# Linear attention and an MLP-mixer block in one program: batch 0's token order, fp32 key transposes, batch 1's numerators, and a new order table

## The chip, the core and the metric

The kernel runs on one core of a Trainium2 chip. A core has five engines that run side by side, each with its own instruction queue: TensorE (PE: matmuls from SBUF into PSUM, with weight loads, PEld, beside them), VectorE (DVE), ScalarE (ACT), GpSimd (POOL) and SyncE (SP), which here only issues transfers. POOL and ACT issue transfers too. The metric is the time of one execution on the device in microseconds (us); lower is better.

## The reference

Eight batches, eight heads, 576 tokens, head size 64, 128 random features. The attention is linear: queries and keys become positive features, and the sum over tokens is taken once for each head. Its result, with the heads side by side (512 channels), goes through a mixer block: an MLP over the tokens (576 to 256 to 576) with a residual, then one over the channels (512 to 1536 to 512) with a residual.

```python
def phi(x):
    proj = np.einsum('bhsd,md->bhsm', x, omega)
    sq = np.sum(x * x, axis=-1, keepdims=True) / 2.0
    h = proj - sq
    h = h - np.max(h, axis=-1, keepdims=True)
    return np.exp(h) / np.sqrt(m)
q_p, k_p = (phi(q_s), phi(k_s))
kv = np.einsum('bhsm,bhsd->bhmd', k_p, v)
z = np.sum(k_p, axis=2)
num = np.einsum('bhsm,bhmd->bhsd', q_p, kv)
den = np.einsum('bhsm,bhm->bhs', q_p, z)[..., None] + 1e-06
# attention out: num / den; then, x being (batch, tokens, channels):
h = np.maximum(xt @ w_tok1, 0.0) @ w_tok2      # xt: x with tokens last
u = x + h.transpose(0, 2, 1)
h2 = np.maximum(u @ w_ch1, 0.0) @ w_ch2
return (u + h2).astype(np.float32)
```

Inputs and output are fp32 in the chip's main memory.

## The kernel before

**Tiling.** Matmul operands are fp16, sums are fp32 in PSUM. The tokens of a batch are cut into 512 main tokens and 64 tail tokens. A main token stands at partition p and place j with token = 4p + j, so one transfer brings four neighbouring tokens to a partition. The tails of two batches share a partition range, and all eight tails go through the channel MLP as a ninth piece at the end (`channel_mix(B, ...)`).

**Stages of a batch.** First q and k are brought with the head size on the partitions. For batches 0 and 1 TensorE does it: `transposes` and `tail_transposes` (L465, L485) write a PSUM bank, ScalarE or VectorE copies it to `kT` or `qT` (L470, L472, L489). For batches 2 to 7 POOL issues a transfer that casts to fp16 in main memory (L354), and SP two transposing ones (L362). Then `attention`, by pairs of heads:

- kp: key features on TensorE (L611), exp on ScalarE (L494); qp: the same for queries (L625).
- km: VectorE takes the maximum over the features (L637) and its reciprocal; vs: POOL scales v with it (L644).
- kv: TensorE sums over tokens (L657, L664), a copy to `kvsb` (L672).
- num: numerators and denominators on TensorE (L691, L693), then reciprocal and product on VectorE into `x` (L700, L701). Batch 0 does one head at a time in one of six PSUM banks; all others do two heads at once in the only two-bank buffer, `pair`.

The tails have their own smaller steps (kt, L526 and L538 or L494; qt, L586; vbd on POOL, L545 or L571). Then comes `token_mix` (L728 to L748, then a transposing transfer from `u` to `uT`, L753) or, for batch 0, `token_mix_first`: it computes u already transposed, in four blocks of 128 channels (L771, L772: w_tok1; L787: x through an identity matmul; L789: w_tok2; L793: the copy to `uT`). At last `channel_mix`: twelve blocks against w_ch1 (L822; for the first two blocks of batch 0 three quarters ahead, L828, and the last quarter later, L830), relu on ScalarE (L839), then four output pieces against w_ch2 (L855), the residual (L864; batch 0 adds it by an identity matmul, L853, and copies at L861), and the store from SP (L869; L872 for the ninth piece).

In `token_mix_first` the 512 columns of the moving operand w_tok2 are read in the order of (j, p), which is a step of four elements in memory:

```python
def w2_of(tb, j=None):
    rows = w2[:, tb, 0:SM].rearrange("p (c j) -> p j c", j=NJ)
    return rows if j is None else rows[:, j, :]
```

**Start of batch 0.** Keys come as fp32 in four pieces of two heads over the queues of ACT and SP (`load_first`, L377) into space that later holds w_ch2. ScalarE casts each to fp16 (L381), and then they are transposed. Everything else comes over POOL's queue. POOL's transfers are chained in the order in which the code names them (`job.after`): the tails and q and v of batch 0, w_tok1, w_tok2, half of w_ch1, batch 1's k, the other half of w_ch1, batch 1's q and v, the two halves of w_ch2 (L442), and then batch 2.

**The order.** Every step is a job with an engine, an estimated cost, the jobs that it needs, the buffers that it takes and gives, and a key. A planner written in the kernel (`Planner.run`) walks through time with those estimates: on each engine, of the jobs that could begin first, the one with the lowest key comes next. Each engine then runs its jobs in that order. Keys come from tables: `HEAD` for batch 0, one entry for each head or block; `NEAR` for batches 1 and 2; `KEYS` for the rest. `BY` says for some copies of batch 0 whether ScalarE (A) or VectorE (D) does them. Where the planner sees TensorE idle before the first channel mix, it puts in matmuls of zeros (`warm`, L908); they compute nothing that is used.

Of the kernel before, what the change touches and what calls it, by code (L numbers as in the profile page):

```python
# [16 lines left out]
KEYS = {"a": -1.383, "as": 0.1, "t": -0.936, "ts": 0.381, "gv": 2.163, "lt": -2.027, "lv": -2.126, "to": -1.882, "tt": 0.315, "ks": 0.333, "km": 0.498, "vs": -0.625, "l1": -2.543, "kt": -0.025}  # L17
NEAR = {"1": {"a": -1.493, "as": 0.086, "t": -1.525, "ts": 0.0, "gv": -0.107, "km": -1.714, "vs": -0.23, "kt": -0.097}, "2": {"a": -1.272, "as": 0.154, "t": -0.7, "ts": 0.142, "gv": 1.686, "km": 3.516, "vs": 1.881, "lv": -1.598, "lt": -2.533, "kt": 0.06}}
HEAD = {"kp": [-3.838, -3.822, -3.798, -3.404], "ke": [-2.728, -2.927, -2.827, -2.727], "km": [-4.011, -3.564, -4.193, -4.006], "vs": [-3.332, -3.487, -3.03, -3.14], "qp": [-3.503, -3.403, -3.303, -3.203], "qe": [-3.328, -3.374, -3.028, -3.128], "kv": [-3.45, -3.145, -2.92, -3.05], "ko": [-3.015, -2.969, -3.397, -2.755], "n": [-3.199, -3.199, -3.182, -3.099, -2.999, -2.999, -2.899, -2.899], "no": [-3.34, -3.34, -3.24, -3.058, -3.14, -4.038, -3.04, -2.3], "ktm": -3.64, "kt": -5.015, "kte": -3.991, "qt": -3.751, "qte": -4.062, "kx": [-6.595, -5.9, -5.8, -5.7], "kxo": [-6.013, -7.195, -5.8, -5.71], "ktx": -6.15, "ktxo": -5.5, "qx": [-5.449, -2.792], "qxo": [-4.557, -3.081], "qtx": -5.58, "qtxo": -3.371, "t1": [-0.475, -0.755, -0.539, -0.445], "re": [-0.554, -0.394, -0.244, -0.084], "ut": [-0.17, -0.48, -0.32, -0.64], "uo": [-0.453, -0.293, -0.302, 0.017], "vbd": -8.94, "w1": -9.59, "w1t": -9.68, "w2t": -8.94, "wa": -8.32, "wb": -8.79, "w2": -8.13}
BY = {"kx": "DDDD", "ktx": "A", "qx": "AD", "qtx": "D", "ko": "ADDA", "re": "AADA", "uo": "DAAA", "no": "DDDDDDDD"}  # L20
# [157 lines left out]
def kernel(  # L178
# [37 lines left out]
    def sb(shape, dt, name):  # L216
        return pool.tile(shape, dt, name=name)
# [13 lines left out]
    omT = sb([P, M], FP16, "omT")  # L231
    ident16 = sb([P, P], FP16, "ident16")
# [142 lines left out]
    def load_first(h0, h1, eng, key, to):  # L375
        def go():
            (nc.sync if eng == "SP" else nc.scalar).dma_start(  # L377
                out=first_k[:, h0:h1, :], in_=k[0, h0:h1, 0:SM, :].rearrange("h (p j) d -> p h (j d)", j=NJ))
        got = dma(eng, key, 0.37 * (h1 - h0), go, cost=0.47)
        def cast():  # L380
            (nc.vector.tensor_copy if to == "DVE" else nc.scalar.copy)(out=nat["k", 0][:, h0:h1, :], in_=first_k[:, h0:h1, :])  # L381
        job = add(to, 0.6 if to == "DVE" else 0.5, key + 0.1, cast, deps=[got])
        for h in range(h0, h1):
            ld["k", 0, h] = job

    def identities():
        make_identity(nc, ident16)
    j_ident = add("POOL", 0.45, -9.9, identities)
    j_om = [dma("SP", -9.95, 0.1, lambda: nc.sync.dma_start(out=omega_nat, in_=omega))]
    load_first(0, 2, "ACT", -9.9, "ACT")  # L390
    load_first(2, 4, "SP", -9.9, "ACT")
    load_first(4, 6, "ACT", -9.7, "ACT")
    load_first(6, 8, "SP", -9.7, "ACT")
# [27 lines left out]
    def w2_of(tb, j=None):  # L421
        rows = w2[:, tb, 0:SM].rearrange("p (c j) -> p j c", j=NJ)
        return rows if j is None else rows[:, j, :]
# [35 lines left out]
    def transposes(b, w, h0, h1, key, on_act=False, key_out=None):  # L459
        name = ("t", w, b, h0)  # L460
        def go():
            ps, ident = bank16(name), ident16
            for i in range(2 * (h1 - h0)):
                h, pr = h0 + i // 2, i % 2
                nc.tensor.transpose(ps[:, i * P : (i + 1) * P], nat[w, b][:, h, pr * P : (pr + 1) * P], ident)  # L465
        def out_():
            n = h1 - h0
            ps = bank16(name)[:, 0 : n * R].rearrange("p (h r) -> p h r", h=n)
            if on_act:
                nc.scalar.copy(out=rows_of(b, w)[:, h0:h1, 0:R], in_=ps)  # L470
            else:
                nc.vector.tensor_copy(out=rows_of(b, w)[:, h0:h1, 0:R], in_=ps)  # L472
        take = [("bank", name)]
        take.append((w + "T", b))
        t = add("PE", mm(2 * (h1 - h0), P) * 1, key, go, deps=[ld[w, b, h0], j_ident], take=take)
        e = add("ACT" if on_act else "DVE", 0.1 + 0.21 * (h1 - h0) if on_act else 0.16 + 0.13 * (h1 - h0), key if key_out is None else key_out, out_, deps=[t], give=[("bank", name)])
        for h in range(h0, h1):
            tr[w, b, h] = e
# [19 lines left out]
    def attention(b, key, step):  # L498
# [95 lines left out]
        for hp in range(NU):  # L594
# [75 lines left out]
            kv_act = b > 0 or BY["ko"][hp] == "A"  # L670
# [8 lines left out]
            for hs in ((0,), (1,)) if b == 0 else ((0, 1),):  # L679
                n_h = (n_n, hs)  # L680
                at = ("bank" if b == 0 else "pair", n_h)
                def where(n_h=n_h, hs=hs):
                    return bank(n_h).unsqueeze(1) if b == 0 else pair(n_h)
# [35 lines left out]
        return last_x, j_start  # L719

    def token_mix(b, key, step, jx):
# [35 lines left out]
        uT.append(dma("SP", key + step * 0.95, 2.6, ut_dma, deps=ju, take=[("uT", b)], cost=3.5))  # L757
        return jr, uT

    def token_mix_first(b, key, step, jx):  # L760

        jrs, uT = [], []
        for db in range(ND):
# [20 lines left out]
            def ut_(n2=n2, cols=cols):  # L784
                ps, x, r1 = bank(n2), t_x[place("x", b)], t_r1[place("r1", b)]
                for j in range(NJ):
                    nc.tensor.matmul(ps[:, j * P : (j + 1) * P], x[:, j, cols], ident16, start=(j == 0), stop=False, skip_group_check=True)  # L787
                for tb in range(NT):
                    nc.tensor.matmul(ps, r1[:, tb, cols], w2_of(tb), start=False, stop=(tb == NT - 1), skip_group_check=True)  # L789
# [23 lines left out]
    def channel_mix(c, key, jt):  # L813
# [3 lines left out]
        for cb in range(NCB):  # L817
# [20 lines left out]
            def relu(cb=cb, n=n):  # L838
                nc.scalar.activation(out=t_r3[place("r3", c)][:, cb, :], in_=bank(n), func=AF.Relu)  # L839
            jr.append(add("ACT", 0.5, key + 0.5 * cb / NCB, relu, deps=[j1], take=[("r3", c)], give=[("bank", n)]))  # L840
        for j in range(NJ):
            last = c == B and j == NJ - 1
            for hf in range(2 if last else 1):
                n = ("h4", c, j, hf)
                cols = slice(hf * (DM // 2), (hf + 1) * (DM // 2)) if last else slice(0, DM)
                prev = None
                for part in range(3):
# [8 lines left out]
                    prev = add("PE", mm(4, 256 if last else 512) + (mm(4, P) if c == 0 and part == 2 else 0.0), key + 0.5 + 0.5 * (3 * j + part) / 12 + 0.2 * hf, c2,  # L856
# [8 lines left out]
                jo = add("DVE", 0.4 if last else 0.69, k2, oadd, deps=[prev], take=[("o", (c, j))], give=[("bank", n)] + ([("u", c)] if 0 < c < B else []))  # L865
                def store(j=j, cols=cols, last=last):
                    o = t_o[place("o", (c, j))]
                    if c < B:
                        nc.sync.dma_start(out=out[c, 0:SM, :].rearrange("(p j) d -> p j d", j=NJ)[:, j, :], in_=o)  # L869
# [22 lines left out]
    for b in range(B):  # L892
        if b >= NPE:
            load_transposed(b, b + key_of("lt", b), [touched.get(b - 2)])
            load_v_tail(b, b + key_of("lt", b) + 0.02)
            load_v(b, b + key_of("lv", b), [ld["ktt", b]])
# [44 lines left out]
```

The softmax here doesn't subtract the row's maximum and nothing guards it: scores larger than these inputs give would overflow.

## Time and profile before

| What | Value |
|---|---|
| Median of 3 runs | 292.88 us |
| Lowest and highest | 292.81 and 293.12 us |
| The profiled execution: its time | 292.57 us |
| its span, first to last instruction | 290.8 us |
| TensorE busy | 283.9 us, 98% of the span |
| ScalarE, VectorE, POOL busy | 155.9, 145.3 and 90.6 us |
| Mean granted TensorE clock | 0.997 |
| Bytes moved by transfers | 39.57 MB |

The profile is of one execution. Times count from its first instruction. The rows name the engine, the line of the code, the operation, and what it writes and reads; a group's row gives its busy time and the mean duration of one in nanoseconds. The duration of a single matmul includes the time that it takes to run through the array, so it overlaps with the next one; the spacing of matmuls is read from the chain of work that ended last, which gives the start, the length and the count of each piece. Counted as busy are also the matmuls of zeros.

### The profile page before, as it was taken

How to read it: one execution, taken by the hardware profiler on the slowest of the kernel's cores; microseconds unless marked ns; L12 is line 12 of the kernel's file. 1: busy time of each engine (PE TensorE's matmuls, PEld its weight loads, DVE VectorE, ACT ScalarE, POOL GpSimd, SP SyncE). 2: the span in 40 equal slices, each digit the busy share in tenths (PEclk: the TensorE clock that was granted, in tenths of full speed). 3: DMA queues.
4: the chain of work that ended last, by engine and by line, in shares of the span. 5: the costliest groups of instructions: out<-in, count | busy, mean ns of one | idle time of the engine just before them, and what ended most of it. 6: DMA issues, size and time to landing. Idle time of an engine off the chain costs nothing.

```text
span 290.8 us, 5502 instructions
## 1 busy us (share of the span) xinstructions
PE 283.9 (98%) x2210; PEld 141.7 (49%) x2210; DVE 145.3 (50%) x269; ACT 155.9 (54%) x305; POOL 90.6 (31%) x115
## 2 busy tenths in 40 slices
PE   7899999999999999999999999999999999999994
PEld 3465454445544544465445544554455444444443
DVE  4885843558449533756567446646465242111011
ACT  5963992098457553865466636753765501621700
POOL 8995740128006501550165014601421000000000
PEclk9999999999999999999999999999999999999998
DMA  8999999699964996999769976897711033003004
GB/s 192 193 197 195 202 228 172 98 246 175 177 108 108 186 152 125 180 171 202 113 129 182 197 114 113 159 221 115 152 72 39 0 72 147 0 18 144 2 20 124
DMA packets 75737, 39.57 MB, mean 136 GB/s; under 512 B 54976, under 2 KB 70720, under 8 KB 75328
## 3 DMA queue, kind: packets, MB, share of 16 engines
q0 software_dynamic: 24304, 17.43, 41.2%
q1 hardware_dynamic: 50624, 21.01, 32.3%
q10 hardware_dynamic: 784, 0.79, 0.9%
q8 instruction: 17, 0.28, 0.4%
q14 instruction: 8, 0.07, 0.1%
HBM read 35.88 MB, written 16.52 MB: 180 GB/s over the span
## 4 chain that ended last, share of the span: by engine, by line
PE 95%; ACT 3%; DVE 0%; issue 0%; DVEq 0%; ACTq 0%
PE bank L855 33%; PE bank L822 32%; PE bank L745 4%; PE bank L728 4%; PE bank L611 3%; PE bank L657 3%; PE bank L625 2%; PE pair L691 2%; PE bank L908 2%; ACT kp L494 1%; PE bank L789 1%; PE bank L803 1%; PE bank L664 1%; PE bank L465 1%; PE bank L729 1%; ACT qp L494 1%
## 5 line engine op out<-in xcount | busy, mean ns | idle before, releaser
L839 ACT ACTIVATE r<-bank 128x512 f16<-128x512 f32 x108 | 64.5, 602 | 69.8 <-PE bank L822 69.8
L855 PE MATMUL bank<-wc,r 128*128 128x512 f16 (+1 forms) x444 | 101.5, 374 | 0.0
L822 PE MATMUL bank<-uT,wc 128*128 128x512 f16 x376 | 89.5, 379 | 0.0
L855 PEld LDWEIGHTS <-r 128*128 128x128 f16 x444 | 40.8, 98 | 46.9 <-issue 5.1
L822 PEld LDWEIGHTS <-wc 128*128 128x128 f16 x424 | 39.5, 98 | 42.6 <-issue 0.5
L637 DVE TENSOR_REDUCE km<-kp 128x8 f16<-128x1024 f16 x32 | 38.7, 1209 | 9.4 <-ACT kp L494 9.2
L494 ACT ACTIVATE qp<-bank 128x512 f16<-128x512 f32 x64 | 35.2, 620 | 13.4 <-PE bank L625 13.4
L494 ACT ACTIVATE kp<-bank 128x512 f16<-128x512 f32 x64 | 34.4, 610 | 8.9 <-PE bank L611 8.9
L644 POOL TENSOR_TENSOR vs<-v,vs 128x512 f16<-128x512 f16 x32 | 33.4, 1055 | 16.1 <-DVE vs L639 12.1
L864 DVE TENSOR_TENSOR o<-u,bank 128x512 f32<-128x512 f16 x28 | 19.1, 681 | 28.1 <-PE bank L855 28.1
L571 POOL TENSOR_TENSOR vbd<-vt,vbd 128x1024 f16<-128x1024 f16 x7 | 13.4, 1919 | 33.2 <-DVE vbd L562 21.7
L365 POOL COPY ktt<-kT 128x256 f16<-128x256 f16 x6 | 2.4, 396 | 68.4 <-DMA kT<-k 68.4
L701 DVE TENSOR_TENSOR x<-pair,rc 128x640 f16<-128x640 f32 x28 | 23.1, 824 | 1.0
L748 DVE TENSOR_TENSOR u<-x,bank 128x512 f16<-128x512 f16 x28 | 17.4, 682 | 9.1 <-PE bank L745 9.1
L700 DVE RECIPROCAL rc<-pair 128x10 f32<-128x10 f32 x28 | 6.0, 216 | 26.9 <-PE pair L693 26.9
L691 PEld LDWEIGHTS <-qp 128*128 128x128 f16 x256 | 12.8, 98 | 6.1 <-issue 0.7
L736 DVE TENSOR_SCALAR r<-bank 128x512 f16<-128x512 f32 x7 | 4.8, 692 | 19.5 <-PE bank L729 19.5
L728 PE MATMUL bank<-x,w1m 128*128 128x512 f16 x56 | 14.4, 379 | 0.0
L657 PEld LDWEIGHTS <-kp 128*128 128x128 f16 x256 | 10.9, 98 | 5.3 <-ACT qp L494 0.9
L657 PE MATMUL bank<-vs,kp 128*128 128x65 f16 x256 | 13.0, 193 | 0.4 <-ACT qp L494 0.4
L745 PE MATMUL bank<-r,w 128*128 128x512 f16 x56 | 13.2, 379 | 0.0
L611 PE MATMUL bank<-omT,kT 64*128 64x128 f16 x256 | 12.5, 218 | 0.1
(102 smaller groups left out, 267.8 us busy)
## 6 DMA issues: line engine op xcount, KB each, us to landing
out_dram<-o SPq DMA_DIRECT2D x32, 256.0 KB, 2.5
q<-in_q_dram POOLq DMA_DIRECT2D x6, 576.0 KB, 6.5
k<-in_k_dram POOLq DMA_DIRECT2D x6, 576.0 KB, 10.2
wc<-in_moe_w_ch_dram POOLq DMA_DIRECT2D x4, 768.0 KB, 10.3
v<-in_v_dram POOLq DMA_DIRECT2D x6, 512.0 KB, 6.3
r<-in_q_dram POOLq DMA_DIRECT2D x4, 256.0 KB, 7.2
v<-in_v_dram POOLq DMA_DIRECT2D x4, 256.0 KB, 7.2
out_dram<-o SPq DMA_DIRECT2D x5, 128.0 KB, 2.3
```

Source lines behind the costliest of these rows:

```text
L494: nc.scalar.activation(out=out, in_=in_, func=AF.Exp, bias=0.0, scale=1.0)
L611: nc.tensor.matmul(ps[e][:, c : c + M], m[half[e], r, :], omT[half[e]], start=True, stop=True)
L637: nc.vector.reduce_max(out=mx, in_=kpv, axis=AX.X)
L644: nc.gpsimd.tensor_tensor(out=vs[:, :, 0:D], in0=t_v[place("v", b)][:, hh[0] : hh[0] + 2, :].rearrange("p h (j d) -> p (h j) d", d=D), in1 ...
L657: nc.tensor.matmul(ps[:, i, :], kpv[:, 2 * i + j // 2, j % 2, :], vs[:, i * NJ + j, 0 : D + 1], start=(i == 0 and j == 0), stop=False, ski ...
L701: nc.vector.tensor_tensor(out=t_x[place("x", b)][:, :, (2 * hp + hs[0]) * D : (2 * hp + hs[0] + n) * D].rearrange("p j (i d) -> p i j d", ...
L728: nc.tensor.matmul(ps, w1m[:, j, tb * P : (tb + 1) * P], x[:, j, :], start=(j == 0), stop=False)
L745: nc.tensor.matmul(ps, w2_of(tb, j), r1[:, tb, :], start=(tb == 0), stop=(tb == NT - 1))
L822: nc.tensor.matmul(ps, wc1[:, db, cb * P : (cb + 1) * P], moving(db), start=(db == 0), stop=(db == ND - 1))
L839: nc.scalar.activation(out=t_r3[place("r3", c)][:, cb, :], in_=bank(n), func=AF.Relu)
L855: nc.tensor.matmul(ps[:, cols], r3[:, cb, j * P : (j + 1) * P], wc2[:, cb, cols], start=(cb == 0), stop=(cb == NCB - 1))
L864: nc.vector.tensor_tensor(out=t_o[place("o", (c, j))][:, cols], in0=uu[:, cols], in1=bank(n)[:, cols], op=ALU.add)
```

## The change

The change has five parts and a new set of keys.

1. Batch 0's token order: w_tok2 is read as it lies, so the columns of the block are tokens in their own order; the identity matmuls of x write PSUM with a step of four to match. The output rows of batch 0 are then 128 neighbouring tokens for each piece.
2. Batch 0's keys are transposed as fp32, straight from where they landed, with an fp32 identity; the ScalarE casts are left out, and the copy from PSUM reads fp32. The fp16 identity is now a VectorE copy of the fp32 one.
3. The last output piece (of the tails) is split into 384 and 128 columns instead of 256 and 256.
4. Batch 1's numerators take one bank for each head, as batch 0's do.
5. v of batch 2 is issued only after u of batch 1 is complete: a small POOL copy reads u first.

With these, `BY` moves some copies between ScalarE and VectorE (now also relus of batch 0's channel mix, `r0`, and kvsb copies of batch 1, `ko1`; two numerators of batch 0 are scaled on ScalarE, with five activations each), and all key tables change. The planner's code does not.

```diff
-KEYS = {"a": -1.383, "as": 0.1, "t": -0.936, "ts": 0.381, "gv": 2.163, "lt": -2.027, "lv": -2.126, "to": -1.882, "tt": 0.315, "ks": 0.333, "km": 0.498, "vs": -0.625, "l1": -2.543, "kt": -0.025}
-NEAR = {"1": {"a": -1.493, "as": 0.086, "t": -1.525, "ts": 0.0, "gv": -0.107, "km": -1.714, "vs": -0.23, "kt": -0.097}, "2": {"a": -1.272, "as": 0.154, "t": -0.7, "ts": 0.142, "gv": 1.686, "km": 3.516, "vs": 1.881, "lv": -1.598, "lt": -2.533, "kt": 0.06}}
-HEAD = {"kp": [-3.838, -3.822, -3.798, -3.404], "ke": [-2.728, -2.927, -2.827, -2.727], "km": [-4.011, -3.564, -4.193, -4.006], "vs": [-3.332, -3.487, -3.03, -3.14], "qp": [-3.503, -3.403, -3.303, -3.203], "qe": [-3.328, -3.374, -3.028, -3.128], "kv": [-3.45, -3.145, -2.92, -3.05], "ko": [-3.015, -2.969, -3.397, -2.755], "n": [-3.199, -3.199, -3.182, -3.099, -2.999, -2.999, -2.899, -2.899], "no": [-3.34, -3.34, -3.24, -3.058, -3.14, -4.038, -3.04, -2.3], "ktm": -3.64, "kt": -5.015, "kte": -3.991, "qt": -3.751, "qte": -4.062, "kx": [-6.595, -5.9, -5.8, -5.7], "kxo": [-6.013, -7.195, -5.8, -5.71], "ktx": -6.15, "ktxo": -5.5, "qx": [-5.449, -2.792], "qxo": [-4.557, -3.081], "qtx": -5.58, "qtxo": -3.371, "t1": [-0.475, -0.755, -0.539, -0.445], "re": [-0.554, -0.394, -0.244, -0.084], "ut": [-0.17, -0.48, -0.32, -0.64], "uo": [-0.453, -0.293, -0.302, 0.017], "vbd": -8.94, "w1": -9.59, "w1t": -9.68, "w2t": -8.94, "wa": -8.32, "wb": -8.79, "w2": -8.13}
-BY = {"kx": "DDDD", "ktx": "A", "qx": "AD", "qtx": "D", "ko": "ADDA", "re": "AADA", "uo": "DAAA", "no": "DDDDDDDD"}
+KEYS = {"a": -1.353, "as": 0.087, "t": -0.936, "ts": 0.381, "gv": 2.14, "lt": -2.027, "lv": -1.831, "to": -1.942, "tt": 0.315, "ks": 1.1, "km": 0.226, "vs": -0.618, "l1": -0.809, "kt": -0.077}
+NEAR = {"1": {"a": -2.195, "as": 0.095, "t": -1.803, "ts": 0.0, "gv": 0.044, "km": -1.819, "vs": -0.475, "kt": -0.001}, "2": {"a": -1.272, "as": 0.154, "t": -0.769, "ts": 0.144, "gv": 1.686, "km": 3.821, "vs": 1.759, "lv": -1.566, "lt": -1.734, "kt": 0.022}}
+HEAD = {"kp": [-3.838, -3.822, -3.798, -3.404], "ke": [-2.728, -2.927, -2.827, -2.727], "km": [-4.039, -3.592, -4.221, -2.75], "vs": [-3.332, -3.487, -3.196, -3.14], "qp": [-3.203, -3.403, -3.303, -3.503], "qe": [-3.328, -3.374, -3.028, -3.748], "kv": [-3.533, -3.228, -3.003, -3.133], "ko": [-3.081, -3.035, -3.463, -3.354], "n": [-3.199, -3.199, -3.182, -3.099, -2.999, -3.268, -2.999, -2.899], "no": [-4.124, -3.426, -3.326, -3.144, -3.226, -3.426, -3.126, -2.386], "ktm": -3.64, "kt": -5.022, "kte": -3.991, "qt": -3.751, "qte": -4.323, "kx": [-6.213, -5.658, -5.558, -5.458], "kxo": [-5.931, -7.05, -5.718, -4.783], "ktx": -6.15, "ktxo": -5.753, "qx": [-5.449, -2.792], "qxo": [-4.073, -3.081], "qtx": -5.093, "qtxo": -3.371, "t1": [-0.475, -0.755, -0.539, -0.445], "re": [-0.129, -0.781, 0.181, 0.341], "ut": [-0.17, -0.48, -0.104, -0.64], "uo": [-0.099, -0.259, -0.108, 0.211], "vbd": -8.97, "w1": -9.8, "w1t": -9.38, "w2t": -8.94, "wa": -9.39, "wb": -9.17, "w2": -8.13}
+BY = {"kx": "ADDD", "ktx": "A", "qx": "DD", "qtx": "A", "ko": "DADD", "re": "AAAA", "uo": "AADD", "no": "DDADDADD", "r0": "AAAAADAAADAA", "ko1": "DDAA", "r1": "AAAAAAAAAAAA"}
...
+    def touch_u(b, key, ju):
+
+        def go():
+            nc.gpsimd.tensor_copy(out=junk[:, b : b + 1], in_=t_u[place("u", b)][:, NJ - 1, DM - 1 : DM])
+        return add("POOL", 0.15, key, go, deps=ju, give=[("u", b)])
...
-        got = dma(eng, key, 0.37 * (h1 - h0), go, cost=0.47)
-        def cast():
-            (nc.vector.tensor_copy if to == "DVE" else nc.scalar.copy)(out=nat["k", 0][:, h0:h1, :], in_=first_k[:, h0:h1, :])
-        job = add(to, 0.6 if to == "DVE" else 0.5, key + 0.1, cast, deps=[got])
+        job = dma(eng, key, 0.37 * (h1 - h0), go, cost=0.47)
...
-        make_identity(nc, ident16)
-    j_ident = add("POOL", 0.45, -9.9, identities)
+        make_identity(nc, ident32)
+    j_ident32 = add("POOL", 0.45, -9.9, identities)
+    j_ident = add("DVE", 0.2, -9.9, lambda: nc.vector.tensor_copy(out=ident16, in_=ident32), deps=[j_ident32])
...
-    def w2_of(tb, j=None):
-        rows = w2[:, tb, 0:SM].rearrange("p (c j) -> p j c", j=NJ)
-        return rows if j is None else rows[:, j, :]
+    def w2_of(tb, j):
+        return w2[:, tb, 0:SM].rearrange("p (c j) -> p j c", j=NJ)[:, j, :]
...
+        first = b == 0 and w == "k"
         def go():
-            ps, ident = bank16(name), ident16
+            ps = bank(name) if first else bank16(name)
+            what, ident = (first_k, ident32) if first else (nat[w, b], ident16)
             for i in range(2 * (h1 - h0)):
                 h, pr = h0 + i // 2, i % 2
-                nc.tensor.transpose(ps[:, i * P : (i + 1) * P], nat[w, b][:, h, pr * P : (pr + 1) * P], ident)
+                nc.tensor.transpose(ps[:, i * P : (i + 1) * P], what[:, h, pr * P : (pr + 1) * P], ident)
...
-            kv_act = b > 0 or BY["ko"][hp] == "A"
+            kv_act = b >= NPE or BY[("ko", "ko1")[b]][hp] == "A"
...
-            for hs in ((0,), (1,)) if b == 0 else ((0, 1),):
+            alone = b < NPE
+            for hs in ((0,), (1,)) if alone else ((0, 1),):
...
-                    nc.tensor.matmul(ps[:, j * P : (j + 1) * P], x[:, j, cols], ident16, start=(j == 0), stop=False, skip_group_check=True)
+                    nc.tensor.matmul(ps.rearrange("p (c j) -> p j c", j=NJ)[:, j, :], x[:, j, cols], ident16, start=(j == 0), stop=False, skip_group_check=True)
                 for tb in range(NT):
-                    nc.tensor.matmul(ps, r1[:, tb, cols], w2_of(tb), start=False, stop=(tb == NT - 1), skip_group_check=True)
+                    nc.tensor.matmul(ps, r1[:, tb, cols], w2[:, tb, 0:SM], start=False, stop=(tb == NT - 1), skip_group_check=True)
...
+            on_act = c >= NPE or BY[("r0", "r1")[c]][cb] == "A"
+            def relu(cb=cb, n=n, on_act=on_act):
+                o = t_r3[place("r3", c)][:, cb, :]
+                if on_act:
+                    nc.scalar.activation(out=o, in_=bank(n), func=AF.Relu)
+                else:
+                    nc.vector.tensor_relu(out=o, in_=bank(n))
...
-                cols = slice(hf * (DM // 2), (hf + 1) * (DM // 2)) if last else slice(0, DM)
+                cols = (slice(0, 3 * P), slice(3 * P, DM))[hf] if last else slice(0, DM)
...
-                        nc.sync.dma_start(out=out[c, 0:SM, :].rearrange("(p j) d -> p j d", j=NJ)[:, j, :], in_=o)
+                        rows = out[c, 0:SM, :]
+                        rows = rows.rearrange("(p j) d -> p j d", j=NJ)[:, j, :] if c else rows[j * P : (j + 1) * P, :]
+                        nc.sync.dma_start(out=rows, in_=o)
...
-            load_v(b, b + key_of("lv", b), [ld["ktt", b]])
+            load_v(b, b + key_of("lv", b), [ld["ktt", b]] + ([touch_u(1, b + key_of("lv", b) - 0.1, added[1])] if b == NPE else []))
```

## The prediction

> **What bounds the kernel now.** I read the page's engine shares and slices first, then the table by stages, then the chain that ended last, and at last the single rows of the head. The shares and the slices:
>
> ```profile
> PE 283.9 (98%) x2210; PEld 141.7 (49%) x2210; DVE 145.3 (50%) x269; ACT 155.9 (54%) x305; POOL 90.6 (31%) x115
> ...
> PE   7899999999999999999999999999999999999994
> ...
> PEclk9999999999999999999999999999999999999998
> DMA  8999999699964996999769976897711033003004
> ```
>
> TensorE is busy throughout, at full clock. But busy is not useful: line 908 multiplies zeros to fill holes. The table by stages, for all instructions (busy PE, PEld, DVE, ACT, POOL; clock; DMA share), then for line 908 alone:
>
> ```profile
> 7.20:17.00 9.80, 8.28 (x99) 4.56 (x99) 8.04 (x16) 9.80 (x23) 9.23 (x13) 1.00 1.29 196
> 17.00:28.00 11.00, 10.93 (x146) 7.23 (x147) 7.41 (x21) 4.06 (x10) 8.64 (x13) 1.00 1.29 193
> 28.00:45.40 17.40, 17.40 (x189) 9.30 (x188) 11.26 (x21) 16.20 (x35) 9.29 (x10) 1.00 1.25 209
> ...
> 0.00:7.20 7.20, 3.98 (x8) 0.95 (x8) 1.00 0.88 191
> 7.20:17.00 9.80, 2.97 (x11) 0.94 (x11) 1.00 1.29 196
> 17.00:28.00 11.00, 1.19 (x4) 0.34 (x4) 1.00 1.29 193
> ```
>
> All filling lies before 28 us, where the first channel mix starts. From 7.2 to 17 ScalarE has no gap; then TensorE sets the pace. The chain says the same (start, length, what):
>
> ```profile
> 6.30 0.34 PE bank L465 x4
> ...
> 7.20 1.56 ACT kp L494 x3
> ...
> 10.51 0.90 ACT qT L470
> 11.41 1.04 ACT kpt L538 x4
> 12.45 1.95 ACT qp L494 x4
> ...
> 16.39 0.60 ACT qp L494
> ...
> 22.80 0.22 PE bank L787 x4
> 23.02 0.90 PE bank L789 x2
> ...
> 234.21 10.36 PE bank L855 x48
> ```
>
> In the last row 48 matmuls of 512 columns take 216 ns each; after 28 us the chain is such rows back to back. So the end is: filling and idling before the channel mix, plus all real TensorE work, plus the stores. The work before 28.07, at the spacings in the chain: 48 transposes (16 early ones at 0.107, the rest at 0.056) 3.5; 8 of L789 at 0.45, 3.6; 40 of L771/L772 at 0.056, 2.2; 40 kp at 0.041, 1.6; 40 numerators at 0.03, 1.2; kv 1.4; L787 0.9; qp 1.3; others 0.8. Sum 16.5, so some 11.6 us are filling and idling. Starting the channel mix early gains only what shrinks in these 11.6 or in the work: postponed work is still paid.
>
> **The change, part by part.**
>
> *Contiguous w_tok2.* L789 reads its moving operand with a step of four fp16 and takes 0.45 us; a contiguous one takes 0.216. Eight of them save 8 x 0.234 = 1.9 us, in a stretch where TensorE is full. In return the 16 identity matmuls of L787 (0.056 each) write PSUM with a step of four fp32. No row shows such a write. The Trainium skill (Advanced Engine Details and Errata, Memory Cachelines) speaks against this trade: SBUF lines are 16 bytes and two hits on a line give full speed, so the old read (8-byte step) should have been free, while in PSUM (8-byte lines) any non-contiguous access slows matmuls. By that rule the saving is 0 and the edit costs time. The row decides the first half: the read does cost 2.1x. For the write, between no penalty (0) and a fourfold time (16 x 0.168 = 2.7), I take the factor of the nearest row, the strided read, about 2x: +0.9. Net -1.0; by the rule, +0.9.
>
> *Keys transposed in fp32.* Four ScalarE casts go (0.62 each, 2.5). The fourth waited for a landing at 6.7 and stood in ScalarE's queue before the first exp: its matmuls were done at about 6.3, it started at 7.20. New path: the first keys land at 3.8 (3.1 after issue, the shortest of L377); four fp32 transposes; a copy from fp32 PSUM (0.62 on ScalarE, 0.69 on VectorE, by the rows of this shape, against 0.42 before); kp 0.4; first exp near 6.0: 1.2 us earlier. No row shows an fp32 transpose. The early fp16 ones stand 0.107 apart (the chain's 0.43 for four). The skill's FP8 and Floating Point Precision (TensorE Precision Notes) gives true fp32 four passes: 16 x 0.43 = 6.8 us; TensorE: Matmul & The Clock Gate (Terms) says transpose mode is four times faster for fp32, so one pass, 1.7 us. I take twice the early row, 0.21 each or 3.4 us: it replaces filling (3.98 us before 7.2), so its cost is 0 in time, between -0.1 and +2 (the four passes are a rival below). VectorE pays 3 x 0.27 = 0.8 more and 0.2 for the fp16 identity; it is idle 4.1 of the first 7.2 us.
>
> *ScalarE's list in 7.2 to 17.* Off it: the first qT copy (0.90) and one kvsb copy (0.3). On it: a q-tail copy (0.4), and two of eight numerators, five small activations each; their nearest row is L538's, 0.26 apart, so 1.3 each. One of them can lie before the last exp. So the last exp comes earlier by 1.2 + 0.9 + 0.3 - 0.4 = 2.0, or 0.7 with a numerator in front. VectorE gets +0.7 and +0.3, loses 0.4 and 2 x 0.49. Against a full gain: km of the last head pair now ranks behind the numerators, and POOL's vs, then kv, wait for it (km 1.43, vs 1.05). I take -1.5 for this stage, bounds -3 and +0.5. From 17 to 28 TensorE holds 9.8 us of work; 1.0 less lets it stay the pace setter: VectorE's last numerator, at 23.1, comes earlier with the stage and by the two that left.
>
> *What the keys move on the queues.* POOL's DMAs are chained in one fixed order, so w1, w_ch1 and batch 1 land as before: the second half of w_ch2 at 28.6 + 13.7 = 42.2. That is a wall for the second matmul of batch 0, which starts at 45.4: 3.2 us of room, of which I use 2.5. The q and k casts of batch 2 may fall behind batch 1's POOL work; they stand behind w_ch2 in the transfer queue until 42.2 anyway, and their two SP transposes land by 52.9, first used at 57.5. Cost 0; without that cover, batch 2's attention would be late, with channel mix to do instead.
>
> *v of batch 2 waits for u of batch 1.* It went out at 53.5, u is ready at 55.1: 1.6 us of delay. Behind the new POOL wait stand v's issue (0.97), the touch of uT and batch 3's casts (62.0). v took 6.5 to land, so 61.6 instead of 60.0; its reader starts at 67.7. uT lands at 61.8 with its reader at 63.7; [...]TensorE waited for neither. 0. If the order puts u later than the old slack of 6 us, batch 2's attention slips behind channel mix: still 0 until TensorE runs out of matmuls.
>
> *Numerators of batch 1 in single banks; kvsb and relu copies to VectorE.* Per head pair 2 x (0.18 + 0.49) instead of 0.22 + 0.82: +0.3, four times 1.2 us on VectorE, which waited 0.9 to 1.7 us before each. Two relus (0.69) and two kvsb leave ScalarE, busy 16.2 of 17.4 there: a help, 0 in the sum since TensorE had no gap. Uncovered, 1.2 us.
>
> *The last piece, 384 + 128 columns.* Matmul time is the same. The last add shrinks from 0.42 to about 0.29, but the 384-column piece is added until about 286.9 and its stores hold SP and ScalarE's queue for 0.5 each, so the last issue stays near 287.5. 0, between -0.15 and +0.15. Contiguous output rows of batch 0 are the same 2 KB rows: 0, with the stores under channel mix.
>
> Sum: -1.0 - 1.5 = -2.5. The profiled execution took 292.57 (span 290.8 and 1.8 around it): 290.1. The median of the runs lies 0.3 above it: 290.4.
>
> **The rivals.**
> 1. *Another engine binds.* The late km, vs, kv chain or the numerators keep the channel mix where TensorE alone would not, and the 1.5 is lost: 292.88 - 1.0 = 291.9. For it: POOL is busy 9.2 of 9.8 us before 17. Against: 1.2 us of ScalarE's start is plainly a queue effect.
> 2. *The change doesn't do what it says.* The strided PSUM write takes back what the contiguous read saves (0.17 us for each of 16, where I took 0.11) and the stage gain goes into filling: 292.9, within 0.6.
> 3. *Slower: fp32 transposes in four passes.* At 0.43 each all 16 need 6.8 us on TensorE, so from 3.9 to 11.5 with two kp between. Both q transposes queue behind: qp exps from about 14.3, eight of them 4.1, the last kp exps and qpt 1.5, so the last exp ends at 19.9 instead of 18.0: +2.0, less the 1.0 of w_tok2: 293.9. It decides from about 0.3 us a transpose. Against: from 6 us on fp16 transposes already stand 0.056 apart, not 0.107.
>
> **How the numbers follow.** My forecast, gains of 1.3 to 4 us: 0.68. Rival 1, gains of 0.6 to 1.3: 0.15. Rival 2: 0.07. Rival 3: 0.10. About 0.2%, 0.6 us, is what this measurement can tell from no change. So faster 0.83, same 0.07, slower 0.10. Low end: the stage gains its 3, the PSUM write costs little: 292.9 - 1.9 - 2.4 = 288.6. High end 292.2: into rival 1 up to its upper edge, leaving out rivals 2 and 3 and a little below, just under 2 in 10.
>
> **What would show it.** Right: the rows of L789 at 0.216 us a matmul, L787 below 0.12; fp32 transposes about 0.2 apart; first exp near 6 and last exp before 17; the first channel-mix matmuls (L828 before, at 28.07) by 26, filling down by a microsecond or more, TensorE without a gap afterwards, the second matmul of batch 0 just after 42.2. Wrong: fp32 transposes above 0.3 apart, L787 above 0.17, new filling between 17 and 26, or idle TensorE near 42.

## The result, and the profile after

The changed kernel takes 291.41 us (median of 4 runs, 290.87 to 291.60) against 292.85 (4 runs, 292.68 to 293.12): a ratio of 0.9947, with an interval of 0.993 to 0.9964. The gain is 1.4 us where 2.5 were forecast: the direction is right, and the size is too large. The profiled execution took 291.6 us, its span 289.8; against the profiled one of before that is 1.0 us less, so the traces account for 1.0. The other 0.4 is how the two profiled executions lie about their medians (0.3 below, 0.2 above); the changed kernel was profiled once more later (experiment 5), and that span was 289.4, 1.4 less.

The engine shares and slices of the changed kernel:

```profile
PE 283.2 (98%) x2207; PEld 143.6 (50%) x2207; DVE 147.9 (51%) x280; ACT 153.3 (53%) x307; POOL 91.0 (31%) x116
...
PE   8999999999999999999999999999999999999993
...
PEclk9999999999999999999999999999999999999999
DMA  8999999799975997999767976998511043012014
```

Nothing to see at this scale: TensorE is as full as before, and the difference is less than one slice. The table by stages (busy PE, PEld, DVE, ACT, POOL; clock; DMA share), first for all instructions, then for the matmuls of zeros, which are now line 925:

```profile
7.20:17.00 9.80, 9.30 (x124) 5.24 (x125) 9.37 (x19) 9.44 (x23) 9.27 (x12) 1.00 1.29 193
17.00:28.00 11.00, 10.94 (x160) 8.55 (x157) 6.71 (x18) 5.89 (x20) 8.59 (x13) 1.00 1.28 193
28.00:45.40 17.40, 17.08 (x176) 9.14 (x175) 14.66 (x34) 14.34 (x30) 9.38 (x10) 1.00 1.26 211
...
0.00:7.20 7.20, 3.37 (x7) 0.81 (x7) 1.00 0.87 193
7.20:17.00 9.80, 3.38 (x12) 1.05 (x12) 1.00 1.29 193
17.00:28.00 11.00, 0.38 (x1) 0.10 (x1) 1.00 1.28 193
```

Three things are to be seen. Filling before 28 us fell from 8.14 to 7.13. Between 7.2 and 17 it did not fall at all (2.97 before, 3.38 now), so TensorE still had room there; VectorE is now busy for 9.37 of 9.80 us, where it was 8.04. And TensorE, full before from 28 to 45.4, now has 0.3 us of gaps there. The chain of work that ended last (start, length, what):

```profile
4.79 2.41 PE bank L471 x12
7.20 0.33 PE bank L617 x8
7.53 0.59 PE bank L471 x4
...
8.79 0.51 ACT kp L500
...
11.18 1.21 ACT kpt L544 x4
12.39 0.49 ACT kp L500
12.88 0.97 ACT qp L500 x2
...
15.74 0.96 ACT qp L500 x2
...
21.54 0.44 PE bank L797 x4
21.97 0.43 PE bank L799 x2
...
28.45 1.59 ACT kp L500 x3
30.03 0.99 ACT r L852 x2
...
275.02 10.40 PE bank L870 x60
...
285.52 0.29 DVE o L879
```

Twelve fp32 transposes in a row stand in front of the first eight kp matmuls, so the first exp starts at 7.56 us, where 7.20 was the old time and 6.0 the forecast. From 8.79 to 16.70 the chain is ScalarE's list, as before; the part on the prediction comes back to this. The trade of w_tok2 is two rows: L797, the identity matmuls that now write with a step, 0.11 each; L799, the contiguous read, 0.216 each. At 28 to 31 us TensorE waits for ScalarE's exps and relus. At the end TensorE finishes 1.50 us earlier (285.42 against 286.92), but the span ends only 1.0 earlier: the tail gives back 0.5.

The times at which the head passes its marks, from the traces (us). "Copy 4" is the start of VectorE's copy of the fourth and last piece of keys; "lag" is from there to the second channel-mix matmul of batch 0 (L870), from which on the work is the same (from there to the start of TensorE's last matmul it is 241.4 us in every row). A number in brackets is the experiment:

| Kernel | keys 4 land | copy 4 | first exp | channel mix | second matmul | lag |
|---|---|---|---|---|---|---|
| before | 6.66 | 7.79 | 7.20 | 28.00 | 45.27 | 37.48 |
| after | 6.89 | 8.15 | 7.56 | 25.76 | 43.77 | 35.62 |
| w_tok2 alone (1) | 7.29 | 8.42 | 7.84 | 27.70 | 44.97 | 36.55 |
| even end (3) | 7.32 | 8.05 | 6.64 | 25.61 | 43.62 | 35.56 |
| after, again (5) | 7.08 | 7.82 | 6.93 | 25.37 | 43.37 | 35.56 |
| casts, same order (6) | 7.23 | 8.58 | 7.78 | 27.76 | 45.77 | 37.19 |
| second kp first (7) | 7.29 | 8.09 | 6.78 | 25.64 | 43.65 | 35.56 |
| numerators on VectorE (8) | 7.07 | 7.92 | 7.32 | 25.80 | 43.96 | 36.05 |
| even end, no wait (9) | 7.02 | 7.75 | 6.77 | 25.38 | 43.38 | 35.63 |
| fp32 transposes twice (10) | 7.26 | 9.96 | 8.94 | 27.52 | 45.53 | 35.56 |
| even end, two fillings fewer (11) | 6.97 | 8.01 | 7.41 | 25.60 | 43.60 | 35.60 |

### The profile page after: what moved, and what is told of

Read it like the earlier page. It is cut to its first block, busy times and chain, and to the rows that moved or that the text cites. A ratio compares the mean times of both kernels' runs of the same rounds, so it can differ in the third digit from the quotient of the medians.

```text
span 289.8 us, 5517 instructions
## 1 busy us (share of the span) xinstructions
PE 283.2 (98%) x2207; PEld 143.6 (50%) x2207; DVE 147.9 (51%) x280; ACT 153.3 (53%) x307; POOL 91.0 (31%) x116
## 4 chain that ended last, share of the span: by engine, by line
PE 93%; ACT 3%; DMA 1%; issue 0%; DVE 0%; DVEq 0%
PE bank L870 33%; PE bank L832 31%; PE bank L737 4%; PE bank L754 4%; PE bank L617 3%; PE bank L663 3%; PE bank L631 2%; PE pair L698 2%; PE bank L471 2%; ACT kp L500 1%; PE bank L813 1%; PE bank L670 1%; PE bank L738 1%; ACT qp L500 1%; DMA omega_nat<-in_omega_dram 1%; PE bank L781 1%
## 5 line engine op out<-in xcount | busy, mean ns | idle before, releaser
L870 PE MATMUL bank<-wc,r 128*128 128x512 f16 (+2 forms) x444 | 101.5, 374 | 0.0
L852 ACT ACTIVATE r<-bank 128x512 f16<-128x512 f32 x106 | 63.4, 602 | 70.3 <-PE bank L832 69.7
L870 PEld LDWEIGHTS <-r 128*128 128x128 f16 x444 | 40.4, 98 | 47.5 <-issue 5.1
L577 POOL TENSOR_TENSOR vbd<-vt,vbd 128x1024 f16<-128x1024 f16 x7 | 13.5, 1928 | 26.9 <-DVE vbd L568 23.3
L708 DVE TENSOR_TENSOR x<-pair,rc 128x640 f16<-128x640 f32 x24 | 19.8, 824 | 0.8
L707 DVE RECIPROCAL rc<-pair 128x10 f32<-128x10 f32 x24 | 5.2, 215 | 22.4 <-PE pair L700 22.4
```

The source lines that it names most:

```text
L708: nc.vector.tensor_tensor(out=t_x[place("x", b)][:, :, (2 * hp + hs[0]) * D : (2 * hp + hs[0] + n) * D].rearrange("p j (i d) -> p i j d", ...
L852: nc.scalar.activation(out=o, in_=bank(n), func=AF.Relu)
L870: nc.tensor.matmul(ps[:, cols], r3[:, cb, j * P : (j + 1) * P], wc2[:, cb, cols], start=(cb == 0), stop=(cb == NCB - 1))
```

## The experiments

My theory was that the head's stage was lost at its start, where TensorE's queue holds the first kp matmuls back. The rival was that another engine paces the head whatever the first exp does; a third question was what the tail costs. Ratios are to the kernel before in the same set of runs.

**1. The w_tok2 trade alone**, in the kernel before (batch 0's output rows are stored to match):

```diff
-nc.tensor.matmul(ps[:, j * P : (j + 1) * P], x[:, j, cols], ident16, ...)
+nc.tensor.matmul(ps.rearrange("p (c j) -> p j c", j=NJ)[:, j, :], x[:, j, cols], ident16, ...)
...
-nc.tensor.matmul(ps, r1[:, tb, cols], w2_of(tb), ...)
+nc.tensor.matmul(ps, r1[:, tb, cols], w2[:, tb, 0:SM], ...)
```

> The kernel before with one edit: batch 0's w_tok2 block reads w_tok2 as it lies and the identity matmuls write PSUM with a step of four; every engine's order stays that of before. Theory 1 (the trade is worth what the profile of after shows, 8 x 0.23 saved and 16 x 0.053 paid, and the stretch from 17 to 28 us is paced by TensorE): 1.0 us less than before, near 291.85, and the last product with w_tok2 ends 1.0 earlier than its 27.6 us. Theory 2 (the order or VectorE paces that stretch): under 0.4 us.

Measured: 292.25 us, ratio 0.997 (0.9958 to 0.9982), a gain of 0.8. In its trace the lag is 0.93 shorter. The forecast's net 1.0 holds.

**2. The casts put back, order planned anew:**

```diff
+def cast():
+    nc.scalar.copy(out=nat["k", 0][:, h0:h1, :], in_=first_k[:, h0:h1, :])
+job = add("ACT", 0.5, key + 0.1, cast, deps=[got])
...
-first = b == 0 and w == "k"
+first = False
```

> The changed kernel with its second part undone: ScalarE casts batch 0's keys to fp16 and they are transposed as fp16; the keys of the order stay, so the planner lays the head out anew. Theory 1 (the fp32 transposes gained nothing, since the first key matmul stands behind twelve of them in TensorE's queue and the first exp starts at 7.56 instead of 7.20): within 0.5 us of the changed kernel, first exp between 7.0 and 7.6. Theory 2 (they gained the stage): slower than the changed kernel by 1 us or more.

Measured: 296.58 us, ratio 1.0129 (1.0098 to 1.016). This says little about the casts. Every key was kept, but other jobs now came first, and the waits of TensorE show what that did (waited for, total, times, longest):

```profile
PE bank L634 <- DMA qT<-q: 1.6, 1, 1.6
...
PE bank L474 <- ACT kp L503: 1.2, 1, 1.2
```

A job placed ahead of its data costs more than the edit under test. From here on, a kernel that changes one thing in the head keeps the order of after, instruction by instruction, except where it is said.

**3. The last piece split evenly again (256 and 256):**

```diff
-cols = (slice(0, 3 * P), slice(3 * P, DM))[hf] if last else slice(0, DM)
+cols = slice(hf * (DM // 2), (hf + 1) * (DM // 2)) if last else slice(0, DM)
```

> The changed kernel with the last piece split 256 + 256 again, nothing else moved. Theory 1 (the uneven split made the end longer: from TensorE's last matmul to the end of the span 4.36 us after against 3.86 before, because the wide piece's stores still hold ScalarE's queue): 0.3 to 0.5 us faster than the changed kernel, about 291.0. Theory 2 (as I predicted, the split is worth nothing and the 0.5 is the spread of landings from run to run): within 0.15.

Measured: 290.66 us, ratio 0.9923 (0.991 to 0.9935). The change gains 0.7 us if its own third part is undone. The adds and stores of the ninth piece, before, after and in this kernel (durations in ns, least, median and most, then first and last start):

```profile
L864 DVE TENSOR_TENSOR o<-ut,bank x3: 414/422/690, 285.2 to 287.0; 128x256 f32<-128x256 f16 x2, 128x512 f32<-128x512 f16 x1
L872 ACTq DMA_DIRECT2D out_dram<-o x3: 497/547/743, 285.9 to 287.5; - x3
```

```profile
L879 DVE TENSOR_TENSOR o<-ut,bank x3: 286/553/689, 284.1 to 285.5; 128x512 f32<-128x512 f16 x1, 128x384 f32<-128x384 f16 x1, 128x128 f32<-128x128 f16 x1
L889 ACTq DMA_DIRECT2D out_dram<-o x3: 547/559/748, 284.8 to 286.3; - x3
```

```profile
L889 ACTq DMA_DIRECT2D out_dram<-o x3: 498/548/750, 284.3 to 285.8; - x3
```

The last add did shrink, from 0.42 to 0.29. But the one ahead of it grew to 0.55 and ends 0.20 us after the last matmul starts, where it ended 0.42 before that start in the kernel before. Its store on ScalarE's queue, issued 0.30 after that matmul's start, takes 0.75, and the very last one is issued at 1.14 after it instead of 0.83. It lands at 3.50 instead of 3.04. From the last matmul's start to the end of the span it is 4.61 us, and 4.11 to 4.15 in every kernel with even halves; the kernels with uneven ones have 4.51 to 4.66.

**4. The first kp matmuls ahead of the third key piece, no filling there, order planned anew:**

```diff
+pieces[2].deps.append(started[0])     # the third key piece waits for the first kp
...
-if free:
+if free and not 2.8 < at["PE"] < 4.7:
```

> The changed kernel with the third fp32 piece of keys made to wait for the first key matmuls, and without filler matmuls between 2.8 and 4.7 us of the planner's clock; the planner lays the rest out anew. Theory 1 (TensorE's queue order held the first exp): first exp at 6.0 to 6.6 instead of 7.56, and if ScalarE's list paces the head the end comes 0.5 to 1 us earlier, near 290.7. Theory 2 (later data or VectorE set the head anyway): first exp earlier, end within 0.3 of the changed kernel.

Measured: 293.22 us, ratio 1.0009 (1.0002 to 1.0017). The first exp did come early, at 6.39, and nothing was gained. It doesn't settle the matter: the new plan put all 32 kp matmuls of batch 1 ahead of the channel mix, where none of them stood in after, and the channel mix starts at 28.45 instead of 25.76.

**5. The changed kernel once more**, beside the next three:

> The changed kernel unaltered, beside the next three. Against the kernel before: 0.9930 to 0.9964, as in its first runs; from TensorE's last matmul start to the end of the span 4.6 us again, against 4.15 before, if the uneven split is the cause; if the longer end was the chance of one run, 4.1 to 4.2. The fp32 transposes: 12 in 2.6 us as in the first profile or 1.6 as in the run with the even end[...].

Measured: 291.39 us, ratio 0.9951 (0.9938 to 0.9964): the first result again, with the first exp at 6.93. From the last matmul's start to the end it is 4.56 us, so the longer end is not the chance of one run.

**6. Casts and fp16 transposes in the order of after:**

```diff
-ps = bank(name) if first else bank16(name)
-what, ident = (first_k, ident32) if first else (nat[w, b], ident16)
+ps, what, ident = bank16(name), nat[w, b], ident16
+if first:
+    nc.scalar.copy(out=nat[w, b][:, h0:h1, :], in_=first_k[:, h0:h1, :])
```

> The changed kernel with ScalarE's four fp16 casts back in front of the key transposes, every queue's order otherwise kept exactly (the planner's list is recorded and then issued). Theory 1 (fp32 transposes are worth next to nothing because the head waits for the last key piece, which lands at about 7, and for the queries): within 0.3 us of the changed kernel, last exp before 18.2. Theory 2 (the casts cost ScalarE 2.5 us in the stage that it paces): 1 us or more slower than the changed kernel, last exp near 19.

Measured: 292.49 us, ratio 0.9991 (0.9982 to 1.0), with single runs from 291.35 to 293.59. By the medians the fp32 path is worth 1.1 us in this order. But the profiled run is the slowest of them, and in its head TensorE runs at half the later rate until about 13.5 us, so that qp's exps wait 1.12 us for it:

```profile
9.76 1.03 PE L621 MATMUL bank<-omT,kT 64*128 64x128 f16 x16
...
11.77 2.53 PE L929 MATMUL bank<-zeros 128*128 128x512 f16 x7
...
14.65 1.08 ACT L504 ACTIVATE qp<-bank 128x512 f16<-128x512 f32 x2 [1.12 <-PE bank L635]
```

Of these seven matmuls of 512 columns the first five start 0.43 apart and the last two 0.22; in the changed kernel the seven at this place start 0.21 to 0.28 apart. One run, at 291.35, lies within the range of the changed kernel. How much of the 1.1 belongs to the casts and how much to the rate stays open.

**7. The second pair's kp ahead of the fourth key piece**, the rest of the order kept (kp(0,1) and its two exps moved forward, their banks exchanged):

> The changed kernel's order with one move: the second pair's key matmuls go ahead of the fourth fp32 piece in TensorE's queue (with their banks swapped, so that neither waits for the other), and its two exps ahead of the key tail's copy in ScalarE's. Theory 1 (ScalarE's list is held by the landing of the fourth piece, at about 7, and paces the stage): third exp at 7.5 to 8.1 instead of 8.5 to 8.8, last exp and the start of batch 0's second matmul 0.4 to 0.7 us earlier. Theory 2 (queries, vs or VectorE pace the stage): third exp earlier, the second matmul's start within 0.2.

Measured: 291.39 us, ratio 0.995 (0.9938 to 0.9961). The third exp starts at 7.75 instead of 8.79 (8.30 in the trace of experiment 5), and the end does not move. With two exps out of its way, ScalarE soon stands and waits for VectorE's maxima of the key tails (kt_nb):

```profile
10.86 1.14 ACT L548 ACTIVATE kpt<-pair,kt_nb 128x128 f16<-128x128 f32 x4 [0.26 <-DVE kt_nb L542]
```

The lag is 35.56, as without the move. An earlier supply of exps is worth nothing.

**8. The two numerators on ScalarE given back to VectorE**, the order kept: one multiplication by the broadcast reciprocal in place of five activations.

```diff
-for j in range(NJ + 1):
-    nc.scalar.activation(out=..., in_=..., func=AF.Copy, scale=t_rc[hp % 2][:, i, j : j + 1])
+nc.vector.tensor_tensor(out=..., in0=..., in1=t_rc[hp % 2][:, i].unsqueeze(2).broadcast_to((P, NJ + 1, D)), op=ALU.mult)
```

> The changed kernel's order, but the two numerators of batch 0 that ScalarE scales with five activations each are scaled by VectorE with one product each, at the same place. Theory 1 (the 1.7 us by which the last numerator comes earlier than before is VectorE's relief): last numerator at about 22.4 instead of 21.4, and batch 0's second matmul 0.5 to 1 us later. Theory 2 (TensorE paces from 17 us on and VectorE has room): second matmul's start within 0.2.

Measured: 291.80 us, ratio 0.9958 (0.9946 to 0.997), 0.4 slower than after, with intervals that overlap; the lag is 36.05, 0.43 longer, where the other kernels of this order with fp32 transposes differ by 0.07. ScalarE is relieved of 2.3 us and VectorE given 1 us, and the stretch gets longer. ScalarE does not pace it, and VectorE's list, now without idle time from the fourth copy to 21 us, does.

**9. Without the wait of v for u, with the even end:**

```diff
-load_v(b, ..., [ld["ktt", b]] + ([touch_u(1, ...)] if b == NPE else []))
+load_v(b, ..., [ld["ktt", b]])
```

> The changed kernel with the even end (256 + 256) and without the small POOL copy that makes v of batch 2 wait for u of batch 1; the four other queues keep their order. Beside the even end alone (0.9923 of the kernel before, 0.991 to 0.9935). Theory 1 (no queue waits for either transfer, so the wait is worth nothing): within 0.3 us of it, v issued before u is complete, TensorE without a gap between 50 and 64 us. Theory 2 (v beside uT delays batch 1's channel mix): 0.5 us or more slower, with a TensorE gap before batch 1's first matmul against w_ch1.

Measured: 290.69 us, ratio 0.9927 (0.9913 to 0.994), against 290.66 with the wait. It is worth nothing: v is issued at 53.87 without it and at 54.02 with it (experiment 3), because POOL waits there anyway until a transfer lands at 53.3.

**10. Every fp32 transpose of the keys done twice**, order kept:

```diff
-nc.tensor.transpose(ps[:, i * P : (i + 1) * P], ...)
+for _ in range(2 if first else 1):
+    nc.tensor.transpose(ps[:, i * P : (i + 1) * P], ...)
```

> The changed kernel with each of the sixteen fp32 transposes issued twice, all else in the same order: 0.43 us for each pair at the early clock, which is the price that my slower rival gave one transpose. Theory 1 (that price shows on the head: the first key matmul and the fourth piece move back): first exp about 8.5 to 9.5, last exp 1 to 2 us later, 292.4 to 293.4. Theory 2 (the busy engine only replaces filling and the clock rises earlier, so it is covered): within 0.5 us of the changed kernel.

Measured: 292.95 us, ratio 1.0 (0.9989 to 1.001), 1.5 us slower than after. Its chain, and VectorE's list with what ended its idle time:

```profile
4.78 3.79 PE bank L473 x24
8.57 0.33 PE bank L619 x8
8.90 1.02 PE bank L473 x8
```

```profile
9.96 0.69 DVE L480 CAST kT<-bank 128x512 f16<-128x512 f32 x1 [0.66 <-PE bank L473]
10.57 1.21 DVE L645 TENSOR_REDUCE km<-kp 128x8 f16<-128x1024 f16 x1
11.82 0.21 DVE L647 RECIPROCAL vs<-km 128x8 f16<-128x8 f16 x1
```

The doubling adds 1.38 and 0.43 us on TensorE. VectorE's fourth copy comes 1.81 later (9.96 against 8.15), the second matmul 1.76 later, and the lag is again 35.56: nothing between absorbed it. The first exp came only 1.38 later (8.94), so the second matmul follows the fourth copy and not the first exp.

**11. Two of the early fillings left out, even end:** the two that stand right before the twelve transposes are deleted from the finished order.

> The changed kernel with the even end, its order kept, and the two filler matmuls between the omega transpose and the first key piece left out (they end at 4.6 to 4.8, the piece lands at 3.9 to 4.1). Theory 1 (VectorE's list, which runs without a gap from about 8.1, when it copies the fourth piece, paces the stage): first exp up to 0.7 us earlier, VectorE's first km unchanged at 8.5 to 8.8, the start of batch 0's second matmul within 0.2 of the even end's 43.6. Theory 2 (the first exp paces): that start 0.4 to 0.7 earlier. It could also be slower, if the clock rises later without the fillers.

Measured: 290.81 us, ratio 0.9926 (0.9914 to 0.9938), the same as with them. The twelve transposes start at 4.09, where those of after start at 4.58, but take 2.79 us from the first start to the last end, where those of after took 2.62 (the chain's 4.79 and 2.41 count from the end of the matmul before) and those of the even end 1.64. The fourth copy starts at 8.01, against 8.05 with the even end:

```profile
4.09 2.79 PE bank L472 x12
```

**12. Batch 1's numerators by pairs again, even end, order planned anew** (`alone = b < 1`):

> The changed kernel with the even end and batch 1's numerators two heads at a time in the one two-bank buffer, as before the change; the planner lays out everything from batch 1 on anew. Theory 1 (TensorE has no gap from 31 us on, so the single banks are worth nothing): within 0.4 us of the even end alone. Theory 2 (the pair buffer makes kv and numerators wait and leaves TensorE without work before w_ch2 lands at 42): 0.5 us or more slower, with gaps between 36 and 46.

Measured: 290.90 us, ratio 0.9931 (0.9919 to 0.9943), which can't be told from the even end alone. Single banks are worth nothing that shows.

The best of all kernels is the change with an even end (experiment 3): 290.66 us, 2.4 below before.

## Why the prediction was right in direction and too large in size

**The w_tok2 trade (forecast -1.0): right.** Its matmuls cost what was said, and alone it gave 0.8 in time and 0.93 in the lag. For the write, 0.109 against 0.056 is a factor of two. The Trainium skill (Advanced Engine Details and Errata, Memory Cachelines) says that a non-contiguous PSUM access slows matmuls, and these rows agree and put the size at two. Its other half, that a read with two hits on a 16-byte line is free, is contradicted: the step of 8 bytes cost 0.45 against 0.216.

**The stage from 7 to 17 (forecast -1.5): the step that failed.** It took ScalarE alone for the pace setter and its first exp for the start. The first exp moved later, not 1.2 earlier: two fillings and twelve transposes were ahead of its matmuls in TensorE's queue, which the step did not count. It would not have mattered. With a first exp anywhere from 6.64 to 8.94, the kernels that kept the changed order, the fp32 transposes and ScalarE's numerators reach the second matmul 35.56 to 35.63 us after copy 4. (Experiment 6, with the casts and the low rate, needs 37.19; there VectorE waits for TensorE after copy 4.) So the start is the transposing of the last keys.

From there on VectorE has next to no idle time up to 17, 0.2 us in all. Before, its first km had still waited for a kp exp:

```profile
8.80 1.22 DVE L637 TENSOR_REDUCE km<-kp 128x8 f16<-128x1024 f16 x1 [0.59 <-ACT kp L494]
```

Now that row has no bracket, and a query copy that was counted as a relief of ScalarE stands in VectorE's list (start, length, what, and in brackets idle time and what ended it):

```profile
8.15 0.69 DVE L478 CAST kT<-bank 128x512 f16<-128x512 f32 x1 [0.23 <-PE bank L471]
8.76 1.21 DVE L643 TENSOR_REDUCE km<-kp 128x8 f16<-128x1024 f16 x1
10.00 0.21 DVE L645 RECIPROCAL vs<-km 128x8 f16<-128x8 f16 x1
10.12 0.70 DVE L538 TENSOR_REDUCE kt_nb<-pair 128x2 f32<-128x256 f32 x2
10.74 0.68 DVE L478 COPY qT<-bank 128x1024 f16<-128x1024 f16 x1
```

Idle time alone doesn't single VectorE out, though: ScalarE has none from 7.56 to 21 either, and the chain above goes over ScalarE. The two lists are nearly equally long. The experiments tell them apart: put ahead, ScalarE waits for VectorE (experiment 7), and relieved at VectorE's expense, it gains nothing (experiment 8). In the kernels of that span ScalarE's last exp ends 9.36 to 9.70 us after copy 4, and the lag differs by 0.07 at most. So the first rival (another engine binds) holds for the cause, and 291.41 lies nearer to its 291.9 than to the forecast's 290.4. It does not hold for the sum, since the order took 0.9 out of the lag. The shift of the second matmul, -1.50, is:

- the last keys landed later, +0.23, and the copy came later after the landing, +0.13 (1.26 against 1.13; it was 0.73 to 0.85 in other runs of this head with its fillings, where the rate of the transposes rose earlier);
- the w_tok2 trade, -0.93, as measured in the order of before;
- the two numerators taken off VectorE, -0.43;
- the rest of the new order, -0.50, by difference and not split further. The new order with none of the edits was not tried.

The stage's own part is thus -0.93 + 0.36 = -0.57, not -1.5. The +0.36 is the chance of one execution: in the second trace of the same kernel copy 4 starts only 0.03 later than before, and the stage's part is about -1.0. The channel mix started 2.24 earlier, but 0.3 of that went into the gaps after 28 us. The other 0.4, by difference, must be work that now comes later; no run shows it alone.

**fp32 transposes (forecast 0.2 each, cost 0): the size right, the cost wrong.** They do take twice the fp16 ones, and so the rival of a fourfold time is out. The Trainium skill (FP8 and Floating Point Precision, TensorE Precision Notes) gives true fp32 four passes; by these rows a transpose of fp32 costs twice, not four times. But they replace little filling (3.98 us before 7.2 became 3.37). They lie on the path to the fourth copy, and experiment 10 shows that time added there is paid nearly in full, 1.5 of 1.8 us. Against the casts that they replace they are still no loss (experiment 6).

**The tail (forecast 0, within 0.15): wrong by +0.5.** The step placed the adds rightly and took 0.5 us for each store of the wide piece. ScalarE's takes 0.75, as the largest of the three already did before (743 ns in the row above), so the last issue comes 0.3 later and lands 0.46 later.

**v's wait and the single banks (0): right,** by experiments 9 and 12. v itself landed at 64.95, where 61.6 was forecast, but at 64.44 without the wait too, and its reader starts at 66.73. The relus on VectorE and the kvsb copies were not tried alone.

**The marks.** Right: L799 at 0.216, L797 below 0.12, transposes 0.2 apart (12 in 2.41), channel mix by 26 (25.76), filling down by 1.0. Wrong: the first exp (7.56), the last exp before 17 (17.85), TensorE without a gap, and the second matmul just after 42.2: w_ch2 landed at 42.43, and 1.3 us of room were left.

Two sums of the forecast are off, neither of them in its 290.4. The work before 28 us counts sixteen transposes at 0.107, but only the first eight stand so far apart, so it is 0.4 too high. The low end, 288.6, takes off 2.4 for a stage that was to gain 3; with 3 it is 288.0.

The sum by the traces: -0.93 - 0.57 + 0.5 = -1.0, the difference of the two spans.

## What to carry to other kernels

Before a stage's gain is counted at the engine that is fullest in it, look for the instruction after which an engine's list runs without idle time: an earlier start elsewhere is worth nothing unless that instruction moves too. Here it was VectorE's copy of the last keys, not ScalarE's first exp. Where two lists run without idle time side by side, neither the idle times nor the chain can say which one holds the other; move work on one of them and see. A shorter last piece makes its neighbour longer, and the neighbour's store stands in the queue ahead of the last one. If a program plans its own order, test an edit with the order held fixed, or the test measures the plan.

## What the runs showed that I had not expected

- An fp32 transpose of 128 columns takes 0.213 us while the fp16 one takes 0.107, and 0.109 once that one takes 0.056: twice, at both rates.
- The rate of the early matmuls changes within a run where the granted clock reads 1.00 throughout (some expectations call it the clock), and the moment differs from run to run of one order. Among the twelve fp32 transposes the step fell from 0.213 to 0.109 after the second in experiment 3, after the sixth in experiment 5, and not at all in the first trace of the changed kernel and in experiment 11: 1.64, 2.00, 2.62 and 2.79 us for the twelve. In experiment 6 the low rate lasted until about 13.5 us. The landing of the last keys, between 6.89 and 7.32 us in the kernels of this order, adds its part: copy 4 lies between 7.75 and 8.15 without any edit that bears on it.
